# The first product of an upward seven lands in the second product's PSUM bank; the order table is written anew

## The chip, the cores and the metric

One core of one Trainium2 chip runs the whole kernel. The metric is device microseconds (us) of one execution; less is better. All times below come from the kernel before.

## The reference, cut to what matters

```python
def reference(x, wqkv, wo, w1, w2, w3, w4):          # x: 2048 x 512, F = 1376
    xn = layernorm(x)
    q, k, v = split(xn @ wqkv)                        # 32 heads of 16
    o = linear_attention(phi(q), phi(k), v)           # phi(t) = where(t > 0, t + 1, exp(t)) + 1e-6
    s = o @ wo
    h = gelu(layernorm(xn) @ w1)
    x1 = xn + token_shift(h) @ w2
    h2 = gelu(layernorm(x1) @ w3) @ w4                # upward: w3, downward: w4
    return x + s * silu(x1 + h2)
```

All matrices are fp32. The kernel splits an operand into a high and a low part and forms a product from three matmuls (high by high, high by low, low by high).

## The kernel before, in words

The 2048 rows are four blocks `b` of 512 (four tiles of 128). PE (TensorE) does the products into eight PSUM banks: four of the pool `mm` and four of the pool `acc`. ScalarE (ACT) and VectorE (DVE) take the results out, split them and build the operands of later products. SyncE (SP) and GpSimd (POOL) issue the transfers.

Many two-by-two block products are done with seven products in place of eight, by the function `seven`. It holds three banks: `pa`, `pb` and `pe`. In `pb` a chain runs: a product goes in, the bank is read, the next product is added on top, and so on (a11 b11, then s2 t2, then s3 t3, then a22 t4). The first two products, a11 b11 in `pb` and a12 b21 in `pa`, together give the first quarter of the result. Each product here is six matmuls of 256 columns.

The upward product (`w3`) of blocks 1 to 3 is the stage `up_late`: for each block, five calls of `seven`, so fifteen in all. In this stage the attention products (`attend_pair`, tiles `pas`, `pbs`, `pes`) and their preparation are done between them. Block 0 goes through `up_pair`, and the second mixer product through `mix2`, both with `seven` too. At the end stands the downward product, `down_late` (tiles `pad`, `pbd`, `ped`).

The order of instructions on every engine is made when the kernel is built. A planner takes the operations with their assumed costs, gives each a due time, and places them; a long table of numbers, `SOONER`, shifts the due time of single operations (place in the program, quarter microseconds). Another table therefore gives another order on all engines, from the first load to the last store. `in_turn` fixes the order of the first loads.

At the start the first four tiles of `k` (banks k0 to k3) are made from `wk` and the transposed input `xt0`, whose parts arrive one after another: `wk_1h` and `wk_1l` are the high and low part of the second chunk of `wk`, `u0_1h` and `u0_1l` those of the second chunk of the input, `wkt` is the running sum over the chunks of `wk`, and `ksum` the product that takes it.

Of the kernel before, what the change touches and what calls it, by code (L numbers as in the profile page):

```python
# [8 lines left out]
F32 = mybir.dt.float32  # L9
F32R = mybir.dt.float32r  # L10
AF = mybir.ActivationFunctionType
ALU = mybir.AluOpType
# [399 lines left out]
def linear_attn_gated_by_mixer(  # L412
# [36 lines left out]
    TH = BT // 2  # L449
# [25 lines left out]
    def bank(name):  # L475
        return pl.new("mm", name, F32, 512)[:, :]
# [452 lines left out]
    def seven(name, z, prod):  # L929

        pa, pb, pe = (bank(f"{n}{name}").cols(0, TH) for n in ("pa", "pb", "pe"))
        p1, p5, u2 = (pl.new("h", f"{n}{name}", F32, TH).all for n in ("p1", "p5", "u2"))

        def go(ps, x, y, start=True):
            products(ps, prod(x, y), start, more=not start)

        go(pb, "a11", "b11")
        pl.act(p1, pb, AF.Copy)
        go(pa, "a12", "b21")
        pl.tt(z[0], pa, p1, ALU.add)  # L940
        go(pe, "s1", "t1")
        pl.act(p5, pe, AF.Copy)
        go(pb, "s2", "t2", False)
        pl.act(u2, pb, AF.Copy)
        go(pe, "s4", "b22", False)
        pl.tt(z[1], u2, pe, ALU.add)
        go(pb, "s3", "t3", False)
        pl.tt(z[2], pb, p5, ALU.add)
        go(pb, "a22", "t4", False)
        return pb  # L950
# [363 lines left out]
    def up_late(b, s):  # L1314
        at = shelf(HF.setdefault(b, {}), f"h{b}_", QLEFT, "f")
        a11, a12, a21, a22 = (at(q, s)[0] for q in QS)
        ps = seven(f"{b}_{s}", (a11, a21, a22), lambda x, y: [AF3[s][x][c] + YT[b][y][c] for c in range(2)])
        for v in (a11, a21, a22):
            pl.act(v, v, AF.Gelu_apprx_tanh)
# [394 lines left out]
    b = 2  # L1714
# [24 lines left out]
    b = 3  # L1739
# [74 lines left out]
    for b in LINE:  # L1814
# [121 lines left out]
```

## Time and profile before

| what | value |
| --- | --- |
| median of three runs | 498.36 us (498.01 to 498.67) |
| the profiled execution, span from first to last instruction | 496.4 us |
| PE busy | 490.6 us, 99% of the span |
| DVE busy | 438.4 us, 88% |
| ACT busy | 373.4 us, 75% |
| POOL busy | 123.6 us, 25% |
| granted TensorE clock | 0.999 of full speed |

The profiled execution is shown by its span alone, which is 1.96 us under the median of the runs. PE is busy nearly always, but a matmul's row is longer than the step to the next one, since they overlap in the engine; a short hold between two matmuls does not show as idle time. To find one, read from start to start.

### The profile page before, as it was taken

How to read it: one execution, taken by the hardware profiler on the slowest of the kernel's cores; microseconds unless marked ns; L12 is line 12 of the kernel's file. 1: busy time of each engine (PE TensorE's matmuls, PEld its weight loads, DVE VectorE, ACT ScalarE, POOL GpSimd, SP SyncE). 2: the span in 40 equal slices, each digit the busy share in tenths (PEclk: the TensorE clock that was granted, in tenths of full speed). 3: DMA queues.
4: the chain of work that ended last, by engine and by line, in shares of the span. 5: the costliest groups of instructions: out<-in, count | busy, mean ns of one | idle time of the engine just before them, and what ended most of it. 6: DMA issues, size and time to landing. Idle time of an engine off the chain costs nothing.

```text
span 496.4 us, 9885 instructions
## 1 busy us (share of the span) xinstructions
PE 490.6 (99%) x3244; PEld 447.0 (90%) x3244; DVE 438.4 (88%) x874; ACT 373.4 (75%) x845; POOL 123.6 (25%) x214
## 2 busy tenths in 40 slices
PE   8999999999999999999999999999999999999996
PEld 6778888888888999899889999999999999999996
DVE  5998997889989669999999999999999899796864
ACT  5999999677887599999988567765686877565531
POOL 1384404276930232133200021100000000143420
PEclk9999999999999999999999999999999999999999
DMA  7869696999974999999988499984634699599996
GB/s 229 303 187 297 133 296 183 237 287 269 329 220 100 236 310 248 273 252 290 337 268 247 158 194 298 247 262 138 183 114 147 215 336 332 114 226 283 278 224 182
DMA packets 87082, 117.44 MB, mean 237 GB/s; under 512 B 10328, under 2 KB 39160, under 8 KB 87032
## 3 DMA queue, kind: packets, MB, share of 16 engines
q1 hardware_dynamic: 75512, 96.11, 59.6%
q0 software_dynamic: 11520, 20.71, 24.9%
q8 instruction: 25, 0.41, 0.4%
q14 instruction: 25, 0.20, 0.1%
HBM read 72.66 MB, written 39.93 MB: 227 GB/s over the span
## 4 chain that ended last, share of the span: by engine, by line
PE 97%; DMA 1%; SPq 1%; ACT 0%; DVE 0%; issue 0%; ACTq 0%
PE pb L146 12%; PE pbd L146 9%; PE h L146 9%; PE g L146 9%; PE acc L146 6%; PE pe L146 6%; PE pbx L146 6%; PE ped L146 5%; PE pbm L146 5%; PE pbs L146 5%; PE q L146 3%; PE pa L146 3%; PE pex L146 3%; PE k L146 3%; PE pad L146 3%; PE pes L146 2%
## 5 line engine op out<-in xcount | busy, mean ns | idle before, releaser
L225 POOL DMA_DIRECT2D xo<-x1d x12 | 10.9, 950 | 166.2 <-DVE xo L191 118.5
L225 POOL DMA_DIRECT2D th<-in_x x14 | 12.2, 895 | 45.0 <-DVE th L201 23.1
L225 POOL DMA_DIRECT2D o<-xnd x16 | 14.0, 887 | 37.5 <-DVE o L191 13.5
L168 ACT ACTIVATE th<-xo 128x512 f32<-128x512 f32 (+1 forms) x16 | 9.7, 614 | 15.9 <-DVE xo L201 10.1
L225 POOL DMA_DIRECT2D zacc<-ke x12 | 12.9, 1073 | 31.4 <-DMA zacc<-ke 10.4
L191 DVE TENSOR_TENSOR ht<-h,abc 128x512 f32<-128x512 f32 x16 | 11.0, 690 | 7.5 <-PE h L146 7.4
L225 POOL DMA_DIRECT2D xt<-nrow x16 | 14.6, 1288 | 8.4 <-ACT k12h L168 4.1
L196 POOL TENSOR_SCALAR w<-mv 128x4 f32<-128x4 f32 (+2 forms) x10 | 2.5, 254 | 40.7 <-ACT sq L168 40.4
L168 ACT ACTIVATE y<-o,nm,rs 128x512 f32<-128x512 f32 x16 | 12.4, 814 | 0.2 <-POOL nm L196 0.2
L168 ACT ACTIVATE p<-pb 128x256 f32<-128x256 f32 x20 | 7.6, 381 | 5.8 <-PE pb L146 5.4
L168 ACT ACTIVATE ht<-ht 128x512 f32<-128x512 f32 x16 | 10.0, 626 | 2.1 <-DVE ht L191 2.0
L168 ACT ACTIVATE sq<-o,mv 128x512 f32<-128x512 f32 x16 | 11.5, 722 | 0.1
L168 ACT ACTIVATE u<-pb 128x256 f32<-128x256 f32 x20 | 7.7, 383 | 5.1 <-PE pb L146 4.5
L201 DVE SCALAR_TENSOR_TENSOR pq<-pq,rd 128x512 f32<-128x512 f32 x16 | 11.0, 688 | 0.3
L168 ACT ACTIVATE p<-pe 128x256 f32<-128x256 f32 x20 | 7.7, 384 | 4.6 <-PE pe L146 4.1
L201 DVE SCALAR_TENSOR_TENSOR qz<-pq,zb 128x512 f32<-128x512 f32 x16 | 10.8, 682 | 0.0
L1471 DVE TENSOR_REDUCE den<-qz 128x32 f32<-128x512 f32 x16 | 10.8, 679 | 0.0
L168 ACT ACTIVATE sq<-o 128x512 f32<-128x512 f32 x16 | 10.0, 629 | 0.1
L613 POOL TENSOR_TENSOR rs<-w,nhalf 128x4 f32<-128x4 f32 (+2 forms) x10 | 9.7, 970 | 0.8
L168 ACT ACTIVATE x<-x,nm,rs 128x512 f32<-128x512 f32 x12 | 9.2, 805 | 0.0
L201 DVE SCALAR_TENSOR_TENSOR th<-th,so 128x512 f32<-128x512 f32 x12 | 8.2, 683 | 0.6 <-ACT th L168 0.5
L168 ACT ACTIVATE sq<-x,mv 128x512 f32<-128x512 f32 x12 | 8.6, 718 | 0.1
(2075 smaller groups left out, 2446.9 us busy)
## 6 DMA issues: line engine op xcount, KB each, us to landing
w_s<-in_w SPq DMA_DIRECT2D x28, 256.0 KB, 5.6
x<-in_x SPq DMA_DIRECT2D x16, 256.0 KB, 6.2
xt<-in_xt SPq DMA_DIRECT2D x16, 256.0 KB, 6.9
xnd<-x SPq DMA_DIRECT2D x16, 256.0 KB, 5.9
xt<-nrow POOLq DMA_DIRECT2D x16, 256.0 KB, 7.6
pqd<-qr SPq DMA_DIRECT2D x16, 256.0 KB, 6.1
o<-xnd POOLq DMA_DIRECT2D x16, 256.0 KB, 6.6
x1d<-o SPq DMA_DIRECT2D x16, 256.0 KB, 5.1
```

The lines of the kernel that those rows point to most:

```text
L146: lambda: nc.tensor.matmul(out.get(), lhs.get(), rhs.get(), start=start, stop=stop, skip_group_check=more))
L168: nc.scalar.activation(out.get(), src.get(), func, scale=get(scale), **kw)
L191: self.vec(eng, out, [a, b], lambda: self.e(eng).tensor_tensor(out.get(), a.get(), b.get(), op=op), True)
L196: lambda: self.e(eng).tensor_scalar(out.get(), a.get(), get(s1), get(s2), **kw), False,
L201: lambda: self.nc.vector.scalar_tensor_tensor(out.get(), a.get(), get(s), b.get(), op0=op0, op1=op1),
L225: lambda: self.nc.gpsimd.dma_start(out.get(), get(src), accum_op=ALU.add), mb=mb)
L613: lambda: g.tensor_tensor(out.get(), src.get(), nh.get(), op=ALU.pow))
L1471: pl.add("DVE", .6, .68, [t], [den], lambda: nc.vector.tensor_reduce(den.get(), t.get().rearrange("p (h d) -> p h d", d=DH), axis=AX.X, op ...
```

## The change

`seven` gets a second way, used by `up_late` alone. There the tile `pa` is no longer a bank of `mm` but one of `acc`. ScalarE copies a11 b11 out of `pb` not into a buffer `p1` in SBUF but into that bank, and the six matmuls of a12 b21 are added on top of it. The bank then holds the first quarter, and ScalarE's GELU reads it from there. The addition on VectorE that joined the two is gone, fifteen times. In the program the product s1 t1 now comes before a12 b21. The table `SOONER` is another one (the rows below show what it does at three places).

```diff
-    def seven(name, z, prod):
+    def seven(name, z, prod, first=None):
...
-        pa, pb, pe = (bank(f"{n}{name}").cols(0, TH) for n in ("pa", "pb", "pe"))
-        p1, p5, u2 = (pl.new("h", f"{n}{name}", F32, TH).all for n in ("p1", "p5", "u2"))
+        pb, pe = (bank(f"{n}{name}").cols(0, TH) for n in ("pb", "pe"))
+        p5, u2 = (pl.new("h", f"{n}{name}", F32, TH).all for n in ("p5", "u2"))
...
+        if first is not None:
+            pa = pl.new("acc", f"pa{name}", F32, 512).all.cols(0, TH)
+            go(pb, "a11", "b11")
+            pl.act(pa, pb, AF.Copy)
+            go(pe, "s1", "t1")
+            pl.act(p5, pe, AF.Copy)
+            go(pa, "a12", "b21", False)
+            first(pa)
+            go(pb, "s2", "t2", False)
+            pl.act(u2, pb, AF.Copy)
+            go(pe, "s4", "b22", False)
+            pl.tt(z[1], u2, pe, ALU.add)
+            go(pb, "s3", "t3", False)
+            pl.tt(z[2], pb, p5, ALU.add)
+            go(pb, "a22", "t4", False)
+            return pb
+        pa, p1 = bank(f"pa{name}").cols(0, TH), pl.new("h", f"p1{name}", F32, TH).all
...
     def up_late(b, s):
...
-        ps = seven(f"{b}_{s}", (a11, a21, a22), lambda x, y: [AF3[s][x][c] + YT[b][y][c] for c in range(2)])
-        for v in (a11, a21, a22):
+        ps = seven(f"{b}_{s}", (a11, a21, a22), lambda x, y: [AF3[s][x][c] + YT[b][y][c] for c in range(2)],
+                   lambda pa: pl.act(a11, pa, AF.Gelu_apprx_tanh))
+        for v in (a21, a22):
...
-        25, 43, 34, 17, 48, 11, 52, 22, 57, 4, 63, 3, 76, 3, 88, -164, 90, 14, 91, -77, 94, 30, 95, 2, 96, 3,
+        21, 775, 46, 50, 48, -22, 54, 1, 76, 3, 79, -1, 82, -7, 88, -279, 91, -19, 96, 21, 97, 62, 98, -5, 101,
```

VectorE near the start of the program, while the first tiles of `k` are made. Before:

```order
L191 TENSOR_TENSOR wkt_146<-wk_s0_100,wk_s1_118 128x512
L191 TENSOR_TENSOR wk_1l_157<-wk_s1_118,wk_1h_144 128x512
L191 TENSOR_TENSOR wkt_146<-wkt_146,wk_s2_122 128x512
L191 TENSOR_TENSOR u0_1l_173<-xt0_1_120,u0_1h_154 128x256
L191 TENSOR_TENSOR wk_2l_175<-wk_s2_122,wk_2h_162 128x512
```

And in the change:

```order
L191 TENSOR_TENSOR wkt_147<-wk_s0_100,wk_s1_118 128x512
L191 TENSOR_TENSOR u0_0l_143<-xt0_0_106,u0_0h_130 128x256
L191 TENSOR_TENSOR wk_1l_165<-wk_s1_118,wk_1h_158 128x512
L191 TENSOR_TENSOR u0_1l_173<-xt0_1_120,u0_1h_168 128x256
L191 TENSOR_TENSOR wkt_147<-wkt_147,wk_s2_122 128x512
L191 TENSOR_TENSOR wk_2l_186<-wk_s2_122,wk_2h_170 128x512
```

The low part `u0_1l` now stands ahead of the sum that needs the third chunk of `wk` (`wk_s2`), and a part of `u0_0l` that stood later has come ahead of both.

PE at the same place, from the matmuls of k1 with the first chunk on. Before:

```order
L146 MATMUL k1_167<-wk_s0_100,xt0_0_106 128x512
L146 MATMUL k1_167<-wk_1h_144,u0_1h_154 128x512
L146 MATMUL k1_167<-wk_1l_157,u0_1h_154 128x512
L146 MATMUL k1_167<-wk_1h_144,u0_1l_173 128x512
L146 MATMUL k1_167<-wk_2h_162,u0_2h_171 128x512
L146 MATMUL k0_116<-wk_1h_144,u0_1h_154 128x512
```

And in the change:

```order
L146 MATMUL k1_156<-wk_s0_100,xt0_0_106 128x512
L146 MATMUL k3_145<-wk_0l_138,u0_0h_130 128x512
L146 MATMUL k3_145<-wk_0h_126,u0_0l_143 128x512
L146 MATMUL k0_116<-wk_1h_158,u0_1h_168 128x512
L146 MATMUL k1_156<-wk_1h_158,u0_1h_168 128x512
L146 MATMUL k1_156<-wk_1l_165,u0_1h_168 128x512
L146 MATMUL k1_156<-wk_1h_158,u0_1l_173 128x512
```

The first matmul that reads `u0_1l` has one more matmul of the second chunk ahead of it.

PE in the second call of the stage `up_late` (tiles `pb1_1`, `pa1_1`; `pb1_0` belongs to the call before it), from the last matmul of a11 b11. Before:

```order
L146 MATMUL pb1_1_4244<-yb111h_3976,w3_1_al_3206 128x256
L146 MATMUL pb1_0_4205<-yt31h_4119,w3_0_s1h_1859 128x256
L146 MATMUL pb1_0_4205<-yt31l_4179,w3_0_s1h_1859 128x256
L146 MATMUL pb1_0_4205<-yt31h_4119,w3_0_s1l_3160 128x256
L146 MATMUL pb1_0_4205<-yt31h_4119,w3_0_s1h_1859 128x256
L146 MATMUL pb1_0_4205<-yt31l_4179,w3_0_s1h_1859 128x256
L146 MATMUL pb1_0_4205<-yt31h_4119,w3_0_s1l_3160 128x256
L146 MATMUL pb1_1_4244<-yt21h_4101,w3_1_s0h_2145 128x256
```

And in the change:

```order
L146 MATMUL pb1_1_4231<-yb111h_3924,w3_1_al_2797 128x256
L146 MATMUL pb1_0_4188<-yt31h_4107,w3_0_s1h_1897 128x256
L146 MATMUL pb1_0_4188<-yt31l_4224,w3_0_s1h_1897 128x256
L146 MATMUL pb1_0_4188<-yt31h_4107,w3_0_s1l_2791 128x256
L146 MATMUL pb1_0_4188<-yt31h_4107,w3_0_s1h_1897 128x256
L146 MATMUL pb1_0_4188<-yt31l_4224,w3_0_s1h_1897 128x256
L146 MATMUL pb1_0_4188<-yt31h_4107,w3_0_s1l_2791 128x256
L146 MATMUL pa1_1_4259<-yb211h_3594,w3_1_ah_2135 128x256
```

Behind the six matmuls of the neighbour there now stands a12 b21 in `pa1_1`, which waits for ScalarE's copy, where s2 t2 in `pb1_1` stood, which waited for the same copy. This is the call with the fewest matmuls between the two; over the fifteen calls they are 7, 6, 25, 7, 7, 10, 9, 11, 7, 9, 13, 11, 8, 7 and 12.

## Rows read from the trace of the kernel before

**Rows 1.** The page: busy time of PE, and the chain that ended last.

```profile
PE 490.6 (99%) x3244; PEld 447.0 (90%) x3244; DVE 438.4 (88%) x874; ACT 373.4 (75%) x845; POOL 123.6 (25%) x214
...
PE 97%; DMA 1%; SPq 1%; ACT 0%; DVE 0%; issue 0%; ACTq 0%
```

**Rows 2.** Windows by stage: busy us (instructions) per engine, granted clock, DMA share, GB/s.

```profile
285.00:410.00 125.00, 124.93 (x1031) 123.52 (x1030) 120.69 (x252) 87.06 (x220) 7.00 (x8) 1.00 0.75 215
410.00:492.00 82.00, 82.00 (x694) 81.86 (x692) 63.18 (x128) 42.12 (x91) 21.06 (x24) 1.00 0.93 238
```

**Rows 3.** Windows of 25 us within the stage `up_late`, same columns.

```profile
310.00:335.00 25.00, 25.00 (x213) 25.00 (x212) 24.87 (x52) 17.42 (x46) 1.73 (x2) 1.00 0.88 255
335.00:360.00 25.00, 24.93 (x210) 24.61 (x209) 24.75 (x54) 13.93 (x40) 0.00 (x0) 1.00 0.59 162
```

**Rows 4.** Timeline of the start: start us, length us, engine, instruction.

```profile
7.49 0.69 DVE L191 TENSOR_TENSOR wk_1l<-wk_s,wk_1h 128x512 fp32r<-128x512 f32 x1
...
8.27 0.80 PE L146 MATMUL k<-wk_1h,u_1h 128*128 128x512 f32 x1
...
8.57 0.69 DVE L191 TENSOR_TENSOR wkt<-wkt,wk_s 128x512 f32<-128x512 f32 x1 [0.40 <-DMA wk_s<-in_wqkv]
8.90 0.39 PE L146 MATMUL k<-wk_1l,u_1h 128*128 128x512 f32 x1
...
9.18 0.42 DVE L191 TENSOR_TENSOR u_1l<-xt,u_1h 128x256 fp32r<-128x256 f32 x1
...
9.66 0.51 PE L146 MATMUL k<-wk_1h,u_1l 128*128 128x512 f32 x1 [0.37 <-DVE u_1l L191]
```

**Rows 5.** Timelines of DVE and PE where the next operands are due.

```profile
15.74 1.42 DVE L191 TENSOR_TENSOR wqt<-wqt,wq_s 128x512 f32<-128x512 f32 x2
...
18.51 1.02 PE L146 MATMUL qsum<-wqt,ones 128*128 128x512 f32 x2
```

**Rows 6.** Groups of ACT by form, 285 to 410 us: busy us, mean ns, idle before.

```profile
L168 ACT ACTIVATE p<-pb 128x256 f32<-128x256 f32 x15 | 5.7, 383 | 2.9 <-PE pb L146 2.5
...
L168 ACT ACTIVATE h_a110f<-h_a110f 128x256 f32<-128x256 f32 x6 | 2.5, 411 | 0.0
...
L168 ACT ACTIVATE h_a120f<-pb 128x256 f32<-128x256 f32 x6 | 2.3, 381 | 1.2 <-PE pb L146 1.0
```

**Rows 7.** Groups of DVE by form, 285 to 410 us, same columns.

```profile
L191 DVE TENSOR_TENSOR h_a110f<-pa,p 128x256 f32<-128x256 f32 x6 | 2.5, 421 | 0.1
...
L191 DVE TENSOR_TENSOR h_a11xf<-pa,p 128x256 f32<-128x256 f32 x3 | 1.3, 420 | 0.0
```

**Rows 8.** Timeline: a11 b11 ends, is copied, and s2 t2 follows in `pb1_0`.

```profile
294.76 0.28 PE L146 MATMUL pb<-yb111h,w_al 128*128 128x256 f32 x1
...
295.08 0.39 ACT L168 ACTIVATE p<-pb 128x256 f32<-128x256 f32 x1 [0.29 <-PE pb L146]
...
295.58 0.32 PE L146 MATMUL pb<-yt21h,w_s0h 128*128 128x256 f32 x1
...
295.74 0.28 PE L146 MATMUL pb<-yt21l,w_s0h 128*128 128x256 f32 x1
```

**Rows 9.** Timeline at 338 us: PE and its weight load.

```profile
338.24 0.28 PE L146 MATMUL pbs<-m_t2h,q6s0l 128*128 128x256 f32 x1
...
338.58 0.19 PEld L146 LDWEIGHTS pes<-m_b22h,q6s1h 128*128 128x128 f32 x1 [0.27 <-ACT p5s L168]
...
338.81 0.28 PE L146 MATMUL pes<-m_b22l,q6s1h 128*128 128x256 f32 x1
```

**Rows 10.** Timeline at 383 us: DVE's addition, and PE behind it.

```profile
383.16 0.39 DVE L191 TENSOR_TENSOR h_a220f<-pb,p 128x256 f32<-128x256 f32 x1
...
383.60 0.38 PE L146 MATMUL pb<-yt43h,w_b 128*128 128x256 f32 x1
...
383.82 0.28 PE L146 MATMUL pb<-yt43l,w_b 128*128 128x256 f32 x1
```

**Rows 11.** Timeline of the end: the last matmul.

```profile
491.79 0.28 PE L146 MATMUL pbd<-w_l1h,dl1l 96*128 96x256 f32 x1
```

113 rows, old and new, of the table SOONER are left out of this document.

## Prediction, made before the changed kernel ran

> **What bounds the kernel now.** I read the page first. PE is busy for 490.6 us of a span of 496.4, and the chain that ended last lies on PE for 97% [rows 1]. So the change can only win or lose where PE is held. The busy time of PE does not tell that, since neighbouring matmuls overlap. I therefore went to the windows and counted matmuls. From 410 to 492 us there are 694 in 82 us, one per 0.118 us [rows 2], and a full window of 25 us in the stage of the upward sevens has 213, one per 0.117 [rows 3]. That step is PE's pace for 256 columns; a stretch with fewer has been held. From 410 us on nothing is left to win.
>
> Then I read the timeline from start to start and looked for steps longer than the pace. Three places matter.
>
> At the start, `wk_1l` by `u_1h` begins at 8.90 us and the next matmul, which reads `u_1l`, at 9.66 [rows 4]. The step is 0.76 us where its neighbours take 0.23, so 0.53 us are lost. The row names VectorE's `u_1l`. That one began at 9.18, behind the sum `wkt`, which had waited for a transfer until 8.57 [rows 4].
>
> In the stage of the upward sevens (285 to 410 us) I find 14 steps that are 0.025 us or more too long, together about 0.95 us. The window from 335 to 360 has 210 matmuls in place of 213, so 0.35 us of it [rows 3]. The largest is at 338: one start at 338.24, the weight load of the next at 338.58, released by ScalarE's copy of the same bank, the matmul after it at 338.81 [rows 9]. Two paces would be 0.23 us, the two took 0.57, so 0.34 are lost. Another is at 383: the addition on VectorE ends at 383.55, PE starts on its bank at 383.60 and goes on at 383.82, 0.10 us beyond the pace [rows 10]. VectorE is busy for 120.69 of these 125 us, ScalarE for 87.06 [rows 2]: an operand that comes late in this stage comes late from VectorE, or from a round trip through a bank.
>
> Between 12 and 285 us the same reading gives some 0.7 us in a dozen places, none above 0.1. The rest up to the end is a fixed tail: the last matmul starts at 491.79 [rows 11], and what follows it (a SiLU, two steps of VectorE, a store) is untouched.
>
> So all that PE can get back is 0.53 at the start, 0.95 in the stage of the change and 0.7 elsewhere, about 2.2 us. The span is 1.96 us under the median; I take that part as fixed and reckon from 498.36.
>
> **The change part by part.** *The addition.* Fifteen go, by three groups of six, six and three of which two are shown: 0.42 us each [rows 7], 6.3 us of VectorE. None is on PE's path. Its worth is what VectorE's lateness costs PE in the stage. 120.69 busy us fall to 114.4 of 125, so VectorE is not full any more. Of the 0.95 us I count the steps that ended with VectorE (383 is one, another of 0.18 us is at 357), together some 0.4 us, as won. Bounds: nothing, if the new order uses the room to do other work earlier; 0.5, if each of them goes.
>
> *The copy.* ScalarE now writes PSUM from PSUM, which no row shows. A copy from PSUM to SBUF of this shape takes 0.383 us [rows 6]. GELU takes 0.411 from SBUF and 0.381 from PSUM [rows 6], so PSUM as a source is 0.03 cheaper. I take 0.383 for the copy, with 0.35 and 0.42 as bounds. The GELU of the first quarter falls from 0.411 to 0.381, fifteen times, 0.45 us on an engine that has 38 us to spare: nothing on the path. The Trainium skill, ScalarE: Activation LUTs, "Step-by-step: what each stage is for", holds that ScalarE writes PSUM faster than SBUF. No run of before shows such a write; by it the wait below at the tightest call would shrink by some hundredths of a microsecond, and the sum would not show it.
>
> *The new wait.* a12 b21 no longer starts freely: its first matmul waits until the copy of a11 b11 is in its bank. Behind it stands all of PE. What a round trip of PE, ScalarE and PE takes is shown by `pb1_0`: last matmul of the product at 294.76, copy at 295.08, next product at 295.58, held until its second matmul at 295.74 instead of 295.70 [rows 8]. The trip takes (295.74 - 0.117) - 294.76, or 0.86 us. Six matmuls between fill seven paces, 0.82 us, and lose 0.04; seven fill 0.94 and lose nothing. In the changed order the fifteen calls have between 6 and 25 matmuls there, one of them 6. If ScalarE is on time the fifteen new waits cost 0.04 us together. If ScalarE is behind another instruction of 0.4 us in each, they cost up to 15 by 0.4, 6 us. ScalarE's copies of `pb` sat idle for PE for 2.5 us before 15 instances [rows 6], so it is mostly early. I take 0.1.
>
> The chain in `pb` had three such trips before and has them still. The old order has 6 matmuls between four times, the new one once (5, at s3 t3 of the first call, 0.16 lost by the same reckoning) and otherwise 7 or more. The step at 338 came from an attention seven with 4 between; in the stage the new order has none under 6. That is 0.34 plus 0.1 won, against 0.16 and the 0.1 above. With 0.4 from VectorE the stage gains 0.6; bounds -0.5 (a loss) to 0.9.
>
> *The banks.* An upward seven now holds two banks of `mm` and one of `acc`. It frees a bank for the planner but costs no instruction, so it enters only through the order.
>
> *The order at the start.* VectorE's `wk_1l` began at 7.49 and steps are 0.6 us for 512 columns, 0.34 for 256. With a part of `u_0l` ahead, `wk_1l` moves to about 7.8 and `u_1l` begins at about 8.4, ending at 8.8 instead of 9.60. On PE the second chunk begins after the same work as before, at 8.67 (8.27 and the 0.40 by which the fp32 product ahead runs over). `wk_1l` is wanted 0.46 later at 9.13, and has ended at 8.5; `u_1l` at 9.36, and has ended at 8.8. The 0.53 us go. Is it kept? The next operand that can be late is `wqt` for `qsum`: its last sum ended at 17.16, and PE took it at 18.51 [rows 5], so 1.35 us of cover. The new order puts `wqt`'s last step behind two others (some 0.6 and 0.5 us) and still has about 0.3 us. I take 0.53; bounds 0 and 0.6.
>
> *The order elsewhere.* Every place has other neighbours. The old one lost 0.7 between 12 and 285 us and nothing from 410 to 492. I have no row that says the new one does better, and the old one stands near its floor there: I take a loss of 0.2, with a gain of 0.5 and a loss of 1.5 as bounds.
>
> **Sum**: 0.53 + 0.6 - 0.2 = 0.9 us less, so 498.36 - 0.9 = 497.5 us.
>
> **The rivals.**
>
> *All holds go.* 0.53, 0.9 and 0.5: 496.4 us. For it speaks that VectorE gets room in its fullest stage. Against it: some of the dozen small holds of before are in places that the addition doesn't touch.
>
> *The start's gain is given back.* The order that is 0.5 us ahead at 12 us arrives at operands that come from transfers, and from VectorE, which is full from 225 to 375 us; PE then waits there for what it had gained, and only the stage's own gain of some 0.4 us less 0.3 of new holds stays: 498.2 us. For it: VectorE has 4.3 us of idle time in 125 [rows 2]. Against it: between 12 and 285 us PE keeps its pace now with no hold above 0.1.
>
> *The new wait binds (slower).* The first matmul of a12 b21 stands at the head of PE and holds all behind it. If ScalarE's copy is late by 0.2 us on average over the fifteen, 3 us are lost, net 2 us after the gains of 0.9: 500.4 us. It decides from a mean of 0.06 us, where the gain is gone, and from 0.13 it is slower than 0.2%. The step at 338 shows that a missing round trip does hold PE [rows 9]. Against it: at the tightest call the old order already waited for the same copy in the same place, with s2 t2, and lost 0.02. The Trainium skill, PSUM — Partial Sum Buffer, "Engine vs sequencer instructions", says that matmuls start and complete in program order; by that rule, which the trace agrees with, nothing overtakes the waiting matmul.
>
> **How the numbers follow.** A measurement of this kernel can tell about 0.2%, or 1.0 us, from no change: faster is under 497.36, slower above 499.36. The forecast gets 0.45 and spans 496.9 to 498.0, a little over half of it (0.26) under the line, since its centre is near it. All holds gone gets 0.15, all of it faster. Given back gets 0.29, all within. The slower rival, with any other mishap of the order, gets 0.11, of which 0.08 is above the line. That makes 0.41 faster, 0.51 the same, 0.08 slower. The range from 496.5 to 498.6 holds the forecast, the given-back case and two thirds of the all-gone one, and leaves out the slow one.
>
> **What would show it.** At the start the step between `wk_1l` by `u_1h` and `u_1l` should be at the pace, and `qsum` half a microsecond earlier. Between 285 and 410 us VectorE should be near 114 us busy, and windows should have 212 or 213 matmuls; the copies into `pa` should take about 0.38 us and the first matmul of a12 b21 show no release by ScalarE longer than 0.05. It would be wrong if the windows from 12 to 285 us held fewer matmuls for the same work, or if holds behind `pa` came in each call.

## The result, and the profile after

The change is slower, by 0.4%: 500.64 us (median of 20 runs, 498.14 to 503.60) against 498.63 us (20 runs, 497.88 to 500.32) for the kernel before. The ratio is 1.0039, with a 95% interval of 1.0027 to 1.0052. The forecast was 497.5 with a range up to 498.6, so the time lies outside it, on the other side.

The first thing to see is the spread: 5.5 us over twenty executions of one program, where the kernel before has 2.4. The execution that was profiled is the fastest of the twenty (498.14 us, span 496.3). Its page differs little from [rows 1]:

```profile
PE 490.6 (99%) x3244; PEld 445.6 (90%) x3244; DVE 434.4 (88%) x859; ACT 373.6 (75%) x845; POOL 126.4 (25%) x214
...
PE 95%; DMA 2%; SPq 1%; DVE 1%; issue 0%; ACT 0%; DVEq 0%
```

The windows by stage, which answer to [rows 2], with the long middle stage ahead of them (busy us and instructions per engine, granted clock, DMA share, GB/s):

```profile
12.00:285.00 273.00, 272.77 (x1486) 232.57 (x1485) 246.83 (x482) 237.45 (x520) 97.12 (x173) 1.00 0.89 250
285.00:410.00 125.00, 125.00 (x1037) 123.97 (x1036) 117.45 (x239) 89.03 (x226) 6.98 (x8) 1.00 0.74 214
410.00:492.00 82.00, 82.00 (x693) 81.81 (x691) 62.47 (x126) 40.22 (x86) 20.92 (x24) 1.00 0.92 238
```

In the stage of the change PE does 1037 matmuls in place of 1031 and VectorE is busy for 117.45 us in place of 120.69: a gain in that stage is there. Steps that are 0.025 us or more too long add up to some 0.3 us in place of 0.95. (This is the best case: in the seven profiles that follow of this order on the engines, with ScalarE's copies made once, the sum is between 0.3 and 0.8 us.) One of them is the place that the prediction named, s3 t3 of the first call with five matmuls between: two steps (297.31 to 297.70) take 0.39 us, where two paces are 0.23, so 0.16 are lost, as reckoned.

```profile
297.31 0.28 PE L146 MATMUL pb<-yb111h,w_al 128*128 128x256 f32 x1
297.48 0.39 PE L146 MATMUL pb<-yt31h,w_s1h 128*128 128x256 f32 x1
297.70 0.28 PE L146 MATMUL pb<-yt31l,w_s1h 128*128 128x256 f32 x1
```

The copy into the bank and the GELU out of it, by form, against [rows 6] (busy us, mean ns, idle before):

```profile
L168 ACT ACTIVATE pa<-pb 128x256 f32<-128x256 f32 x15 | 5.5, 369 | 3.0 <-PE pb L146 2.8
...
L168 ACT ACTIVATE h_a110f<-pa 128x256 f32<-128x256 f32 x6 | 2.3, 377 | 0.8 <-PE pa L146 0.8
```

The copy from PSUM to PSUM takes 0.369 us; a copy to SBUF took 0.383 [rows 6]. The Trainium skill (ScalarE: Activation LUTs, "Step-by-step: what each stage is for") holds that ScalarE writes PSUM faster than SBUF; these rows agree, by 0.014 us.

The start, against [rows 4] and [rows 5]:

```profile
8.39 0.42 DVE L191 TENSOR_TENSOR u_1l<-xt,u_1h 128x256 fp32r<-128x256 f32 x1
...
8.69 0.40 PE L146 MATMUL k<-wk_1l,u_1h 128*128 128x512 f32 x1
8.92 0.45 PE L146 MATMUL k<-wk_1h,u_1l 128*128 128x512 f32 x1
...
9.44 0.40 PE L146 MATMUL k<-wk_1h,u_1l 128*128 128x512 f32 x1
9.94 0.50 PE L146 MATMUL k<-wk_2h,u_2h 128*128 128x512 f32 x1
...
18.23 1.10 PE L146 MATMUL qsum<-wqt,ones 128*128 128x512 f32 x2 [0.19 <-DVE wqt L191]
```

The step to `u_1l` is at the pace (8.69 to 8.92). The step from 9.44 to 9.94 is 0.27 too long: its operand `u_2h` comes from ScalarE behind `wk_2h`, for which ScalarE had waited for a transfer until 8.95. At `qsum` PE waits for `wqt`, 0.36 us beyond the pace from 17.64. At 18.23 PE is 0.28 us ahead of the kernel before (18.51), not 0.53. This varies from execution to execution: in the eight profiles that follow with this order of PE, `qsum` starts between 17.54 and 18.21 us, seven times by 17.95, that is 0.56 us or more ahead.

So the fastest execution of the change shows the gain of the stage and half of that of the start, and keeps 0.1 us of them by its span (496.3 against 496.4, where the profile of the kernel before is not that of its own fastest execution): 0.3 us go at 68 us, where PE waits for `u_2h`, the rest in smaller steps. What costs most other executions 2 to 5 us is not in it. So others were profiled.

### The profile page after: what moved, and what is told of

The parts are those of the page before. It is cut to its first block, busy times and chain, and to the rows that moved or that the text cites. A ratio compares the mean times of both kernels' runs of the same rounds, so it can differ in the third digit from the quotient of the medians.

```text
span 496.3 us, 9870 instructions
## 1 busy us (share of the span) xinstructions
PE 490.6 (99%) x3244; PEld 445.6 (90%) x3244; DVE 434.4 (88%) x859; ACT 373.6 (75%) x845; POOL 126.4 (25%) x214
## 4 chain that ended last, share of the span: by engine, by line
PE 95%; DMA 2%; SPq 1%; DVE 1%; issue 0%; ACT 0%; DVEq 0%
PE pb L146 11%; PE pbd L146 10%; PE h L146 9%; PE g L146 9%; PE acc L146 6%; PE pe L146 6%; PE pbx L146 6%; PE ped L146 5%; PE pbm L146 5%; PE pbs L146 5%; PE q L146 3%; PE pa L146 3%; PE pex L146 3%; PE pad L146 3%; PE pes L146 2%; PE pem L146 2%
## 5 line engine op out<-in xcount | busy, mean ns | idle before, releaser
L225 POOL DMA_DIRECT2D zacc<-ke x12 | 12.4, 1037 | 31.6 <-DVE xf L191 20.2
L196 POOL TENSOR_SCALAR w<-mv 128x4 f32<-128x4 f32 (+2 forms) x10 | 4.0, 396 | 45.3 <-ACT sq L168 44.9
L201 DVE SCALAR_TENSOR_TENSOR qr<-qe,qi 128x512 f32<-128x512 f32 x11 | 7.6, 689 | 1.0 <-ACT qe L168 0.8
```

The lines of the kernel that those rows point to most:

```text
L196: lambda: self.e(eng).tensor_scalar(out.get(), a.get(), get(s1), get(s2), **kw), False,
L201: lambda: self.nc.vector.scalar_tensor_tensor(out.get(), a.get(), get(s), b.get(), op0=op0, op1=op1),
L225: lambda: self.nc.gpsimd.dma_start(out.get(), get(src), accum_op=ALU.add), mb=mb)
```

## The experiments

### 1 and 2. The change again

No edit: the changed kernel as it is, timed again with a profile of another execution, and a profile of one more.

> The changed kernel as it is, to see where a slower execution loses. Its profiled execution of 496.3 us was the fastest of twenty; the median was 500.64 us, 2.0 us above the kernel before, and the spread 5.5 us. Theory A (the new order hangs on transfers that land at varying times): a slower execution has, somewhere ahead of 285 us or after 410 us, one or a few holds of 1 us or more whose releaser is a transfer or an engine that had itself waited for one; the stage of the upward sevens, 285 to 410 us, keeps its 1037 matmuls within 3. Theory B (the new wait for ScalarE's copy is what varies): the holds are spread over the fifteen sevens, 0.1 to 0.4 us each, and the stage loses 10 matmuls or more.

> The changed kernel once more, for a profile of another of its executions. Theory A: the holds lie at the same places as in the other slower execution, ahead of 285 us or after 410 us, with other lengths. Theory B: they are spread over the fifteen sevens.

Measured: 501.71 us (499.83 to 503.09), ratio 1.0061 (1.0043 to 1.0078); the second look 501.0. The profiled spans are 501.3 and 499.2. The waits of PE from 12 to 490 us in the first of them (us in total, times, longest) are two lines:

```profile
PE pex L146 <- ACT p5x L168: 2.4, 1, 2.4
PE pax L146 <- ACT u_2h L168: 1.2, 1, 1.2
```

The second look has 1.5 and 1.1 us in the same two places, and 0.4 at 469 us (`pad`, behind VectorE's `d_a121l`). The timeline of the first look shows what ScalarE and VectorE had waited for:

```profile
67.64 0.40 PE L146 MATMUL pbx<-wk_1l,u_1h 128*128 128x512 f32 x1
68.57 0.63 ACT L168 ACTIVATE u_2h<-xt 128x512 fp32r<-128x512 f32 x1 [1.37 <-DMA xt<-nrow]
69.25 0.50 PE L146 MATMUL pax<-wk_2h,u_2h 128*128 128x512 f32 x1 [1.22 <-ACT u_2h L168]
...
119.32 0.39 PE L146 MATMUL pbx<-kq_t21h,xs_1l 128*128 128x512 f32 x1
120.04 0.75 DVE L201 SCALAR_TENSOR_TENSOR zi<-pax,rs,p1x 128x512 f32<-128x512 f32 x1 [3.03 <-DMA pqd<-qr]
120.82 0.63 ACT L168 ACTIVATE ke<-zi 128x512 f32<-128x512 f32 x1 [2.98 <-DVE zi L201]
121.36 0.67 ACT L168 ACTIVATE p5x<-pex,ns 128x512 f32<-128x512 f32 x1
122.08 0.80 PE L146 MATMUL pex<-wq_2h,xs_3h 128*128 128x512 f32 x1 [2.38 <-ACT p5x L168]
122.68 0.63 PE L146 MATMUL pex<-wq_2l,xs_3h 128*128 128x512 f32 x1
...
125.24 0.47 PE L146 MATMUL pbx<-kq_t30l,xs_2h 128*128 128x512 f32 x1
```

Both holds begin with a transfer. At 67.6 us `u_2h` waits for the gather that adds `nrow` into `xt2_2`. At 117 us `zi13` wants a buffer from which the store of `qr9` is still reading, and behind `zi13`, in order, stand ScalarE's `ke` and `p5x` and then PE. In the fastest profile `zi13` begins at 116.51 with no wait. The store took 5.3 us to land there, 8.9 here and 8.0 in the second look, where `zi13` waits for 2.2 us.

Steps too long: 67.64 to 69.25 is 1.38 over the pace of 0.23, and 119.32 to 122.08 is 2.53. Behind the second hold the clock is down, as the windows show (PEclk is the figure after POOL):

```profile
12.00:285.00 273.00, 269.40 (x1454) 229.63 (x1453) 242.28 (x472) 235.59 (x516) 97.50 (x173) 0.99 0.87 246
...
122.30:125.00 2.70, 2.70 (x7) 2.12 (x8) 2.70 (x5) 2.70 (x6) 2.62 (x6) 0.50 0.93 303
125.00:130.00 5.00, 5.00 (x23) 4.01 (x22) 4.11 (x8) 1.88 (x4) 4.59 (x15) 0.96 0.96 270
...
285.00:410.00 125.00, 125.00 (x1025) 123.33 (x1024) 117.12 (x237) 86.56 (x221) 6.98 (x8) 1.00 0.72 208
```

Seven steps from 122.08 to 125.24 take 3.16 us where seven paces are 1.63: 1.53 more. Together 5.4 us, and the span is 5.0 above that of the fastest execution, which lost 0.3 at 68 us itself. So these two places are as large as the difference between the two executions; what else differs nearly cancels (`qsum` starts 0.7 earlier here, and the stage takes 0.4 longer).

The stage's window holds 1025 matmuls here and 1031 in the second look: by that count theory A missed and theory B had its sign. But the windows lie at fixed times, and the program is 4.6 us late there (the first matmul of a11 b11 starts at 298.25, at 293.65 in the fastest execution). From that matmul to the first into `pad` it is 118.75 us here, 118.37 in the second look and 118.38 in the fastest, so the stage itself loses 0.4 us at most. The window from 12 to 285 us, in which the prediction wanted a missing matmul as the sign of its failure, holds 1454 of them here, 1486 in the fastest execution and 1493 in the kernel before.

### 3 and 4. The new seven in the old order, and the old seven in the new order

```diff
-        21, 775, 46, 50, 48, -22, 54, 1, 76, 3, 79, -1, 82, -7, 88, -279, 91, -19, 96, 21, 97, 62, 98, -5, 101,
+        25, 43, 34, 17, 48, 11, 52, 22, 57, 4, 63, 3, 76, 3, 88, -164, 90, 14, 91, -77, 94, 30, 95, 2, 96, 3,
```

That is experiment 3: the changed kernel with the table of before, each entry carried over to the same operation. Experiment 4 is the kernel before with the changed table, carried over the other way.

> The new seven, with the order table of before carried over operation by operation (the entries of the additions that are gone drop out). The order is the one of before up to the upward stage and differs from there. Theory A: within 0.2% of before or up to 1 us faster, 497.5 to 498.8 us, with the narrow spread of before (2 us or less). Theory B: as slow and wide as the change, 500 to 501 us.

> The old seven, with the new order table carried over. The order is that of the change up to the upward stage. Theory A: as slow and wide as the change, median 500 to 501 us and a spread of 3 us or more. Theory B: 498 to 499 us, spread 2 us or less.

Measured: 501.86 us (501.65 to 502.15), ratio 1.0072 (1.0060 to 1.0084), for the new seven in the old order; 510.07 us (508.19 to 512.63), ratio 1.0237 (1.0213 to 1.0260), for the old seven in the new one. Each table fits only its own seven, so these two runs do not take the theories apart as they were meant to. What they show is that the new seven has no spread in the old order (0.5 us over five executions), and that it loses there in its own stage: 1003 matmuls from 285 to 410 us in place of 1031. The timeline of that run shows two kinds of hold:

```profile
295.33 0.38 ACT L168 ACTIVATE gf<-a 96x256 f32<-96x256 f32 x1 [1.15 <-PE a L146]
295.61 0.85 ACT L168 ACTIVATE pa<-pb 128x256 f32<-128x256 f32 x2
295.72 0.28 PE L146 MATMUL pb<-yb111h,w_al 128*128 128x256 f32 x1
296.04 0.38 PE L146 MATMUL pa<-yb211h,w_ah 128*128 128x256 f32 x1
...
363.58 0.63 ACT L168 ACTIVATE q10s1h<-q10f 128x512 fp32r<-128x512 f32 x1 [0.95 <-DMA q13d<-q13z]
364.12 0.37 ACT L168 ACTIVATE p<-pe 128x256 f32<-128x256 f32 x1
...
364.54 0.39 PE L146 MATMUL pe<-yb222h,w_s1h 128*128 128x256 f32 x1 [0.71 <-ACT p L168]
```

Here the copy is late, and a12 b21 does wait for it, as the slower rival had it: ScalarE makes it behind `gf`, for which it had waited until 295.33 (the row at 295.61 is two copies, of which the first ends at 295.99), and PE starts at 296.04, 0.32 us after the matmul before in place of 0.12. The largest hold, 0.88 us at 363.5, again begins with a transfer.

### 5 to 7. The two places mended, one at a time and together

The order on PE, VectorE, ScalarE and GpSimd is that of the change. In 5, SyncE issues the loads of `x12` to `x15` (operations 727 to 736) behind the store of `x11` (532). In 6, `zi13` and five tiles after it exchange buffers, so that the one from which `qr9` is stored goes to `x12l`. In 7, both.

```diff
+    MOVES = ((736, 532), (733, 532), (730, 532), (727, 532))
+    SWAPS = (('zi13', 'p31'), ('w1_s0', 'p13'), ('wr_20', 'p22'), ('wr_21', 'p20'), ('wt_11l', 'p2'))
...
+        for n, m in self.MOVES:
+            trail.remove(self.ops[n])
+            trail.insert(trail.index(self.ops[m]) + 1, self.ops[n])
...
+            for t in fresh[n:]:
+                t.place = {mine: other, other: mine}.get(t.place, t.place)
```

> The change, with one thing moved: the four loads of x12 to x15 are issued behind the store of x11 (about 65 us) in place of ahead of the stores of x8 to x11 (56 to 59 us), about where the kernel before issues three of them. The order on PE, VectorE, ScalarE and GpSimd stays that of the change. Theory A (the new order hangs on transfers): the four gathers into xt2 at 55 to 59 us then share the transfer engines with 1 MB less, land in about 6.6 us as before in place of 8.7 to 9.2, u_2h does not wait and the hold of PE at 67.6 us (0.2 to 1.4 us in the profiles of the change) goes; the hold at 119 us stays. So 0.5 to 1.2 us less than the change, about 500.3 us if the change is again at 501.2. Rival (the gathers are slow by themselves, or the loss is spread elsewhere): the hold at 67.6 stays and the time is that of the change.

> The change, with other buffers and no other order: zi13 (VectorE, about 116.5 us) takes a buffer that PE has read last, and the buffer from which the store of qr9 reads goes to x12l, some 4 us later; four tiles between them move on by one buffer. Theory A: VectorE no longer waits for that store to land, so the hold of PE at 119 us (nothing in the fastest profile of the change, 1.7 and 2.4 us in two others) goes, and with it the half clock behind it: 1.5 to 3.5 us less than the change in most executions, about 498.7 us, and a narrower spread. The hold at 67.6 us stays. Rival (that hold only happens in profiled executions, or the next wait takes its place, by x12l or a load behind it): 500.5 us or more.

> The change with both edits, the loads of x12 to x15 later and the other buffer for zi13. Theory A: both holds go in every execution; what is left is the fastest execution of the change less its 0.2 us at 67.6: about 498 us, spread under 1 us, equal to the kernel before or up to 0.2% faster, and a span of about 496 us. Rival (the loss is spread over many places): 500 us or more, slower than the kernel before.

Measured, on one chip, against the kernel before at 498.32 us (30 runs):

| kernel | us | ratio | 95% interval |
| --- | --- | --- | --- |
| 5, loads later | 499.47 (498.35 to 501.09) | 1.0028 | 1.0017 to 1.0039 |
| 6, other buffer for `zi13` | 499.12 (498.09 to 501.55) | 1.0019 | 1.0008 to 1.0031 |
| 7, both | 497.51 (496.65 to 499.43) | 0.9986 | 0.9977 to 0.9995 |

From 6 to 7 the loads are worth 0.33%, 1.6 us; from 5 to 7 the buffer is worth 0.42%, 2.0 us. Each is the worth of one edit where the other is made; the change without either was not timed beside these three. By its ratios of 1.0039 and 1.0061 to the kernel before, both edits together are worth 2.6 to 3.7 us. With both, the change is about as much faster as was forecast. The spread did not fall as expected: 2.8 us (496.65 to 499.43), where less than 1 was.

Why the loads matter is read from the rows of the tiles `x` and `xt` (duration in ns, first and last start, times from issue to landing). In the kernel before (the landing line is that of the gathers, the second row):

```profile
L207 SPq DMA_DIRECT2D x<-in_x x4: 328/512/682, 64.0 to 69.3; - x4
...
L225 POOL DMA_DIRECT2D xt<-nrow x4: 870/1406/1716, 56.6 to 58.4; - x4
...
DMA to landing us min/median/max: 4.5/6.6/8.3
```

In the change:

```profile
L207 SPq DMA_DIRECT2D x<-in_x x4: 382/680/1079, 56.4 to 59.0; - x4
...
L225 POOL DMA_DIRECT2D xt<-nrow x4: 870/1408/1712, 55.3 to 57.1; - x4
...
DMA to landing us min/median/max: 5.9/8.7/11.0
```

In the new order 1 MB of loads, which ScalarE first reads at 72.57, goes out beside the four gathers, and these land 2.1 us later by the median. In experiment 5 they land after 6.7 again and `u_2h` does not wait:

```profile
DMA to landing us min/median/max: 4.6/6.7/7.9
```

Over all thirteen profiles of this document the median is 8.6 to 9.2 in the six in which the loads go out early, and 6.5 to 6.8 in the seven in which they go out late. The Trainium skill, DMA: Bandwidth & Descriptors, "Issuing engines are not separate DMA queues", says that transfers of SyncE and GpSimd run on the same engines and interleave; these rows agree.

In the profile of 6, the store of `qr9`, issued at 110.9, takes 7.7 us to land, and `zi13` starts at 116.82 without a wait. In that of 5, with the old buffer, it takes 6.8 and `zi13` waits for 1.0 us. The first row is from 6, the second from 5:

```profile
116.82 0.75 DVE L201 SCALAR_TENSOR_TENSOR zi<-pax,rs,p1x 128x512 f32<-128x512 f32 x1
...
117.06 0.75 DVE L201 SCALAR_TENSOR_TENSOR zi<-pax,rs,p1x 128x512 f32<-128x512 f32 x1 [0.96 <-DMA pqd<-qr]
```

### 8. The early loads in the kernel before

```diff
+    MOVES = ((736, 385), (730, 385), (733, 385), (727, 385))
```

Operation 385 is the store of `x7`; the loads go out at 56 us as in the change.

> The kernel before, with the one thing of the change that theory A names for 67 us: the loads of x12 to x15 issued right behind the store of x7 (about 56 us), ahead of the stores of x8 to x11, as in the new order. Nothing else moves on PE, VectorE or ScalarE. Theory A: the gathers into xt2 land 2 us later than in the kernel before (8.7 in place of 6.6), PE is held near 67 us, and the time rises by 0.3 to 1.3 us, to about 499.2 us. Rival (the kernel before has slack there, and the change's hold comes from its other order on ScalarE or GpSimd): 498.3 us, no hold near 67.

Measured: 499.05 us (498.12 to 500.49), ratio 1.0018 (1.0009 to 1.0026), from one moved group of four loads. The gathers' landing is back at 8.8, and the timeline has the waits:

```profile
69.45 0.64 ACT L168 ACTIVATE u_2h<-xt 128x512 fp32r<-128x512 f32 x1 [0.78 <-DMA xt<-nrow]
...
71.17 0.50 PE L146 MATMUL pex<-kq_t10h,xs_0h 128*128 128x512 f32 x1 [0.31 <-ACT xs_0h L168]
```

So the early loads make the gathers late in either order. Here the delay reaches PE by ScalarE's next outputs: it is held at 71.17, 0.46 us beyond the pace.

### 9 and 10. A third place, and the mended kernel once more

```diff
-    SWAPS = (('zi13', 'p31'), ('w1_s0', 'p13'), ('wr_20', 'p22'), ('wr_21', 'p20'), ('wt_11l', 'p2'))
+    SWAPS = (('zi13', 'p31'), ('w1_s0', 'p13'), ('wr_20', 'p22'), ('wr_21', 'p20'), ('wt_11l', 'p2'), ('dl1h', 'p67'))
```

> The kernel of e7 with a third buffer exchanged: ScalarE's dl1h (about 463 us) takes the buffer from which the store of th10 reads, not that of th11, whose store is issued some 2 us later; VectorE's d1_s20l, 5 us after dl1h, takes that of th11. The order is the same on every engine. Theory A (waits for transfers are the whole of what varies): in the profiles of the change dl1h waited for such a store for 0.8, 2.3 and 3.4 us, and in the last one PE was then held for 0.5 us at 469. With 2 us more of lead the hold does not come, so the highest times go and the median falls by 0 to 0.3 us: about 497.3 us, spread 1.5 us. Rival (dl1h is never what is late next, and the spread is from elsewhere): the same median and spread as the kernel of e7 in this call.

> The kernel of e7 once more, on this chip: 497.5 us and 0.1 to 0.2% under the kernel before by theory A. The rival, that e7's gain was an accident of that chip: equal to the kernel before or slower.

Measured, beside the kernel before at 498.49 us: 498.23 us (496.84 to 501.22), ratio 0.9997 (0.9981 to 1.0013), with the third exchange; 497.34 us (496.58 to 499.08), ratio 0.9976 (0.9967 to 0.9986), for kernel 7 again. The gain of 7 is repeated. The third edit failed: `dl1h` now waits for the other store just as long, and PE is held behind it.

```profile
464.20 0.64 ACT L168 ACTIVATE dl1h<-hl 96x512 fp32r<-96x512 f32 x1 [3.27 <-DMA out<-th]
...
465.91 0.28 PE L146 MATMUL pad<-wf_b211l,d_a121h 128*128 128x256 f32 x1
466.40 0.39 PE L146 MATMUL pad<-wf_b211h,d_a121l 128*128 128x256 f32 x1 [0.21 <-DVE d_a121l L191]
```

That hold costs 0.48 us with the step behind it, so it does not explain 498.23 by itself. Why the median is higher than that of kernel 7 stays open.

The profile of experiment 10 (span 497.3) shows yet another place: at 136.46 PE waits 1.25 us for GpSimd's `u_3h`, behind a row of GpSimd of 5.58 us at 122.71 where such rows take 0.2 to 1.3. This execution is the slowest of the twelve (499.08). So some spread remains in kernel 7 too, and its cause was not followed.

### 11. The copy made twice

```diff
             op.emit()
+            if op.order in self.TWICE:
+                op.emit()
```

`TWICE` holds the fifteen copies of a11 b11 into the bank; the kernel is otherwise that of 7.

> The kernel of e7, with ScalarE's copy of a11 b11 into the bank of a12 b21 made twice in each of the fifteen calls, so that the bank is ready about 0.3 us later; nothing else is moved. In the profile of the change the first matmul of a12 b21 starts 0.05 us behind the copy where it waits for it, and 0.2 to 2.4 us behind it in the calls in which it does not. Theory A (the new wait binds in no call): what cover there is takes most of it, five or six calls with 0.2 to 0.3 us of cover lose some 0.1 us each and as much again until PE is at its pace, 0.5 to 1.2 us together: about 498.3 us. Theory B (the new wait is what costs the change its time): the copy is on the path of PE in most calls, so fifteen times 0.3, some 4.5 us more: 502 us.

Measured: 499.51 us (499.15 to 502.01), ratio 1.0027 (1.0016 to 1.0039), 2.2 us over kernel 7, which was timed beside it (497.34). The second copy ends 0.40 us after the first. In the fifth call:

```profile
321.59 0.78 ACT L168 ACTIVATE pa<-pb 128x256 f32<-128x256 f32 x2
322.06 0.28 PE L146 MATMUL pbs<-m_t3l,q4s1h 128*128 128x256 f32 x1
322.43 0.39 PE L146 MATMUL pa<-yb211h,w_ah 128*128 128x256 f32 x1
322.65 0.28 PE L146 MATMUL pa<-yb211l,w_ah 128*128 128x256 f32 x1
```

PE starts 0.05 us behind the end of the copies (321.59 + 0.78 = 322.37, plus 0.05) and loses 0.36 us over two steps. Such holds stand in seven calls, 0.10 to 0.35 us each, 1.75 us together; the rest is in steps on `pb` and `pbs` near them. Theory A (0.5 to 1.2 us) had the sign and at most half the size; theory B (4.5) would have cost twice as much. In the profile of the change itself the first matmul of a12 b21 starts 0.20 to 2.39 us behind the end of its copy, and a matmul that waits starts 0.05 behind it; so the new wait binds in no call, and the seven other profiles of this order with one copy have the same distances (none under 0.20). The seven calls with less than 0.4 us of that are the seven that are held here.

## Why the prediction was wrong, point by point

**The addition and the stage: the gain was there, the relief too large.** The steps that are too long fall from 0.95 to 0.3 us; 0.6 less was forecast. VectorE was to fall by 6.3 us, to 114.4 in the stage. It fell by 3.2 there, and by 4.0 over the span for fifteen instructions less (438.4 and 434.4), 0.27 us each. A row of 0.42 overlaps its neighbours: by the prediction's own reading such rows start 0.34 apart, which makes 5.1 us for fifteen; what took the rest is not shown. Fifteen times the row was the wrong sum; the gain did not hang on it. Nor is the 0.6 sure: it is there in the fastest execution, while in the profile of kernel 7 the steps too long add up to 0.8, so only some 0.2 is won.

**The copy and the new wait: right.** 0.369 us where 0.383 was taken with bounds of 0.35 and 0.42, and no call in which ScalarE's copy is late. The slower rival was this wait. It is refuted for the new order, and in the old one it is shown to bind (experiment 3, 295.72 to 296.04), with the condition that the rival gave: ScalarE behind another instruction.

**The start: right in most executions, with an error that cost little.** The hold at `u_1l` went. In the profile of the change 0.28 of the 0.53 us is left at `qsum`, in that of kernel 7 0.62:

```profile
17.89 1.10 PE L146 MATMUL qsum<-wqt,ones 128*128 128x512 f32 x2
```

What the prediction had wrong is the cover at `qsum`: it left `wqt` some 0.3 us, and in seven of the nine profiles with this order of PE there is none: PE is held there by 0.07 to 0.44 us. And the prediction did not look at `u_2h` (0.27 late at 9.94), which hangs on a transfer.

**The order elsewhere: this is the step that failed.** It was put at a loss of 0.2 us with 1.5 as the worst case, "I have no row that says the new one does better". It lost 1.6 us by the loads and 2.0 us by the buffer of `zi13`, by experiments 5 to 7, and 2.6 to 3.7 us together. The sum without these two losses is some 0.9 less than before, and the kernel without them is 0.8 us (497.51 against 498.32) and 1.15 us (497.34 against 498.49) faster. So the terms that were worked out hold as a sum; that they do is in part luck, since in the profile of kernel 7 the start gives 0.1 more than its term and the stage 0.4 less. The term that was only estimated decided the sign.

Two things were wrong in that estimate. It came from the holds of the kernel before, as if a new order could only lose what the old one loses; but an order that is free of holds says nothing about the next one. And it was one number, where the cost varies from execution to execution: the store that `zi13` waits for lands after 5.3 us (no wait) or 8.9 (a hold of 2.5 us and 1.5 more at a lower clock). The rival "the start's gain is given back" named operands that come from transfers, and then let PE lose there only what it had gained, some 0.5 us. Nothing caps it at that.

Could it have been seen? The rows of before had the length of a landing. Of the twelve stores `pqd<-qr` from 45.9 to 120.7 us the profile tells it for four, 2.1, 4.4, 7.7 and 8.4 us:

```profile
DMA to landing us min/median/max: 2.1/6.1/8.4
```

In the change's order `zi13` starts 5.9 us behind the store from its buffer (issued at 110.62, `zi13` at 116.51 in the fastest profile). That is less than the median of those four. The kernel before has such a distance too: there it is `x14l` that takes the buffer of `qr9`, at 114.2, behind a store issued at 108.37, and neither its profile nor the two others with that order there (experiments 3 and 8) show a wait. So a short distance is a risk and not yet a loss; what a wait would cost at `x14l` no run shows. Behind `zi13` stand ScalarE and PE. The loads of `x12` to `x15` could be seen in SyncE's new order: they stand ahead of the stores of `x8` to `x11`, where before all four stood behind the first three of these.

## What to carry to other kernels

When the order of a full kernel is made anew, compare SyncE's and GpSimd's issues first: for each buffer that is taken again after a store, and each operand that a gather fills, set the distance in the new order against the longest landing time in the trace, not the median, and look at which transfers are newly in flight together. Executions that spread by more than those of the old kernel can be a sign of such a wait: profile again until a long one is caught. And a table of priorities belongs to one program: the new seven was 3.6 us over the kernel before in the old order, the old seven 11.8 us in the new one.

## What had not been expected of the hardware

The same 256 KB store, in the same place of the program, took 5.3 to 8.9 us to land in the nine profiles of the change and its mended forms (5.3, 5.3, 6.8, 7.5, 7.6, 7.7, 7.8, 8.0, 8.9). And a hold of 2.5 us in a PE that is otherwise always busy cost 1.5 us more behind it: the granted clock was 0.50 of full speed, its lower level of 1.2 GHz, from 122.3 to 125.0 us, and the seven steps there, of 512 columns each, took 0.60 us for the first and 0.43 for the others in place of 0.23. One execution shows this; the hold of 1.4 us at 67.6 had no such tail, nor had that of 1.7 us at 119 in the second look.
